# Four PSUM banks by turns, head-by-head maxima and a new order of slots in a fused routing attention and feed-forward kernel

## The chip, the core and the metric

The kernel runs on one core of a Trainium2 chip. Five engines work side by side, each through its own list of instructions in order: TensorE (PE, matrix products; its weight loads appear as PEld), VectorE (DVE), ScalarE (ACT), GpSimd (POOL), and SyncE (SP), which here only issues transfers. They wait for each other through semaphores. Matrix products are written to PSUM, which this kernel divides into eight banks; all else is in SBUF. The metric is the device time of one execution in microseconds (us). The kernel before takes 1357.56 us, the median of three runs (1356.3 to 1358.26).

## What is computed

An attention block with 4 batches, 8 heads, 768 positions and head width 64, and then a feed-forward block on its 3072 x 512 result. A query sees only the keys that fall to the same one of 16 centroids:

```python
q_assign = np.argmax(np.einsum('bhsd,hcd->bhsc', q_n, c_n), axis=-1)
k_assign = np.argmax(np.einsum('bhsd,hcd->bhsc', k_n, c_n), axis=-1)
mask = q_assign[:, :, :, None] == k_assign[:, :, None, :]
scores = scale * np.matmul(q, k.transpose(0, 1, 3, 2))
scores = np.where(mask, scores, -1000000000.0)
scores = scores - np.max(scores, axis=-1, keepdims=True)
attn = np.exp(scores)
attn = attn / (np.sum(attn, axis=-1, keepdims=True) + 1e-09)
out = np.matmul(attn, v)
# ... and then, x being out as (3072, 512):
h = x @ w_in                                                # 512 -> 2048
sp = np.maximum(h, 0.0) + np.log1p(np.exp(-np.abs(h)))      # softplus
return (h * erf(sp)) @ w_out                                # 2048 -> 512
```

q, k, v and the centroids arrive as 32-bit floats. The two weight matrices arrive as 64-bit floats and are rebuilt as 32-bit ones on the chip.

## The kernel before

The kernel works on pairs of heads, 16 of them, four to a batch. A pair has 12 **units**, each a block of 128 keys against half of the queries (384), for both heads. The parts that matter:

The memory pools in PSUM. A tile of ps_s takes two banks, all others take one, so these pools are all eight banks:

```python
ps_s = pool("ps_s", 2, space=PSUM)     # sc (scores) and sm (maxima)
ps_v = pool("ps_v", 1, space=PSUM)     # av, attention times v
ps_t = pool("ps_t", 1, space=PSUM)     # psim, pn, psum: small things
ps_f = pool("ps_f", 2, space=PSUM)     # hp, po: feed-forward; av2
```

The weights are rebuilt in 32 **steps**, 16 for w_in and 16 for w_out. Each has a load, ACT's absolute value, two POOL operations (clamp and bias), and five DVE instructions, one to a call of `prepare(1)`:

```python
def clamp(n):
    ae.activation(out=x, in_=hi, func=ACT.Abs)
    ge.tensor_scalar(out=x, in0=x, scalar1=TINY_HI, scalar2=None, op0=ALU.max)
    ge.tensor_tensor(out=x, in0=x, in1=bias.to_broadcast([P, LC]), op=ALU.add)
def convert():
    ...
        ve.tensor_scalar(out=m, in0=x, scalar1=3, scalar2=None, op0=ALU.logical_shift_left); yield
        # ... fetch of a later step
        ve.tensor_scalar(out=x, in0=m, scalar1=0x7F800000, scalar2=None, op0=ALU.bitwise_and); yield
        # ... clamp of a later step
        ve.scalar_tensor_tensor(out=xf, in0=lo, scalar=2.0**-52, in1=xf, op0=ALU.mult, op1=ALU.mult); yield
        ve.tensor_tensor(out=xf, in0=mf, in1=xf, op=ALU.add); yield
        ve.scalar_tensor_tensor(out=w_steps[n][0], in0=hi, scalar=0x80000000, in1=x, ...); yield
```

`route(p)` finds the clusters of pair p and writes one-hot rows into the operands qm and km, which add the mask to the scores; `shift(p)` finds each query's maximum and writes its negative into one row of qm. Both are prepared while the pair before is worked on (`aside`):

```python
def route(p):                       # each yield ends one portion
    # DVE: transposes of q and k -> qT, kT; load of the next pair
    yield
    # PE: psim = similarities; ACT: copies of qT, kT into qm, km
    yield
    ve.transpose(out=sims, in_=psim)
    ve.reduce_max(out=mx, in_=sim, axis=AX.X)
    ve.tensor_tensor(out=sim, in0=sim, in1=mx..., op=ALU.is_equal)
    ge.tensor_tensor(out=sim, in0=sim, in1=rank..., op=ALU.mult)
    # ACT: the row of shifts is set to 0
    yield
    ve.reduce_max(out=mr, in_=sim, axis=AX.X)
    # DVE: hot (two halves), hotT = its transpose; DVE -> qm, ACT -> km
    yield
def shift(p):
    for t in range(NJ):             # 6 blocks of queries
        for half in range(2):       # halves of the keys
            sm = ps_s.tile([P, 2, 512], F32, name="sm", tag="s")
            for e in range(2):      # the two heads
                te.matmul(sm[:, e, 0:HW], lhsT=st["qm"]..., rhs=st["km"]..., start=True, stop=True)
            ve.tensor_reduce(out=nmx[:, t, half], in_=sm[:, :, 0:HW], axis=AX.X, op=ALU.max, negate=True)
            yield
    # nm = min of both halves (DVE), pn = its transpose (PE), nmT (ACT),
    # and through DRAM (line) into the row of qm, all queries at once
    yield
```

A unit is scored (`scores`: products into sc, exponential into pr by ACT, the sum acc over units by POOL), multiplied with v two units later (`attend`: av) and divided after six (`divide`: psum by PE, logarithm and exponential by ACT, den and xT by DVE). The feed-forward has 12 chunks of 256 positions: `hidden` fills hp, DVE copies it to g; `gate` multiplies g with erf(softplus(g)); `project` fills po, which DVE copies to osb:

```python
def gate(n):
    for i in range(2): ae.activation(out=s[i], in_=h[...], func=ACT.Softplus)
    for i in range(2): ae.activation(out=s[i], in_=s[i], func=ACT.Erf)
    for i in range(0, NFT, GW):     # eight pieces
        ve.tensor_tensor(out=h[:, i : i + GW], in0=s[...], in1=h[:, i : i + GW], op=ALU.mult)
```

The first batch is laid out in slots, in which every engine keeps the order of the program; from slot FIRST on a scheduler may move instructions, and the feed-forward (`pump`) is mixed in:

```python
FIRST = 2 * NJ * HP - 4
for slot in range(-2 * NJ, 2 * NJ * HP):     # -12 .. 47; one unit to a slot
    in_order[0] = slot < FIRST
    p, r = divmod(slot + 2 * NJ, 2 * NJ)
    if slot >= 0:
        scores([slot])
    if r == 0:
        ready[p] = aside(p)
    prepare(3 if slot < 0 else (1, 3, 1)[r] if r < 3 else 3 if r > 9 else 0)
    for _ in range(1 if r < 4 or r == 10 else 2 if r < 10 else 0):
        next(ready[p])
    if slot >= 2:
        # ... second part of an earlier divide
        attend(slot - 2, ...)
        # ... divide after six units
    if slot >= FIRST:
        pump(4 * NFT * TB)
```

After it, units 48 to 191 go two at a time; each two have five rounds of `pump(per_slot)`, `prepare(2)` and, where ASIDE lists the round, one portion of the next pair's preparation. What is left of the feed-forward runs at the end.

Of the kernel before, what the change touches and what calls it, by code (L numbers as in the profile page):

```python
# [17 lines left out]
P = 128  # L18
# [11 lines left out]
GW = 2  # L30
# [13 lines left out]
ASIDE = (0, 2, 4, 6, *range(9, 9 + 2 * NJ), 10 + 2 * NJ)  # L44
FIRST = 2 * NJ * HP - 4
# [19 lines left out]
def kernel(  # L65
# [33 lines left out]
    ps_v = pool("ps_v", 1, space=PSUM)  # L99
    ps_t = pool("ps_t", 1, space=PSUM)  # L100
    ps_f = pool("ps_f", 2, space=PSUM)
# [51 lines left out]
    load_qk(0)  # L153
# [42 lines left out]
    room = [gp.tile([P, NFT, TB], F32, name="g") for _ in range(2)]  # L196
# [3 lines left out]
    def fetch(n):  # L200
        if n in steps or n >= len(w_steps):
            return
        if n < n_w_in:
            t = room[n // 2 % 2][:, n % 2 * (NFT // 2) : (n % 2 + 1) * (NFT // 2)]
        else:
            t = half_tile()
        t = t.rearrange("p f t -> p (f t)").bitcast(U32)
        nc.sync.dma_start(out=t[:, 0 : 2 * LC], in_=w_steps[n][1])
        raw = t[:, 0 : 2 * LC].rearrange("p (n w) -> p n w", w=2)
        steps[n] = raw[:, :, 1], raw[:, :, 0], t[:, 2 * LC : 3 * LC], t[:, 3 * LC : 4 * LC]  # L210
# [53 lines left out]
    for n in range(3):  # L264
        fetch(n)
# [33 lines left out]
    pct = ps_t.tile([P, P], F32, name="pct", tag="t")  # L299
# [12 lines left out]
    def route(p):  # L312
# [9 lines left out]
        psim = ps_t.tile([P, HW], F32, name="psim", tag="t")  # L322
# [21 lines left out]
        )  # L344

# [3 lines left out]
        for e in range(2):  # L349
            row = low["q"][e * D + SH : e * D + SH + 1, e]  # L350
            ae.mul(out=row, in_=row, mul=0.0)
# [11 lines left out]
        ve.transpose(out=hotT, in_=hot)  # L363
        for half in range(2):
            cols = slice(half * HW, (half + 1) * HW)
            for e in range(2):
                r = slice(e * D, e * D + Q)
                g = slice(half * Q, (half + 1) * Q)
                ve.tensor_scalar_mul(out=low["q"][r, e, cols], in0=hotT[g], scalar1=own[g, e : e + 1])
                g = slice(D + half * Q, D + (half + 1) * Q)  # L370
                ae.copy(out=low["k"][r, e, cols], in_=hotT[g])
# [4 lines left out]
    def shift(p):  # L376
        st = pairs[p]
        nmx = small.tile([P, NJ, 2, 2], F32, name="nmx")
        load(p, "v", v, vp)
        for t in range(NJ):  # L380
            for half in range(2):
                sm = ps_s.tile([P, 2, 512], F32, name="sm", tag="s")
                for e in range(2):
                    te.matmul(
                        sm[:, e, 0:HW], lhsT=st["qm"][:, e, t * P : (t + 1) * P],
                        rhs=st["km"][:, e, half * HW : (half + 1) * HW], start=True, stop=True,
                    )
                ve.tensor_reduce(
                    out=nmx[:, t, half], in_=sm[:, :, 0:HW], axis=AX.X, op=ALU.max, negate=True
                )  # L390
                yield
        nm = small.tile([P, 2, NJ], BF16, name="nm")
        ve.scalar_tensor_tensor(
            out=nm.rearrange("p e t -> p t e"), in0=nmx[:, :, 0], scalar=FLOOR, in1=nmx[:, :, 1],
            op0=ALU.min, op1=ALU.min,
        )
        pn = ps_t.tile([2 * NJ, P], BF16, name="pn", tag="t")
        te.transpose(out=pn, in_=nm.rearrange("p e t -> p (e t)"), identity=identb)
        nmT = small.tile([2 * NJ, P], BF16, name="nmT")
        ae.copy(out=nmT, in_=pn)  # L400
        line = linep.tile([2 * NJ, P], BF16, name="line")
        nc.sync.dma_start(out=line, in_=nmT)
        for e in range(2):
            r = e * D + SH
            nc.sync.dma_start(
                out=st["qm"][r : r + 1, e],
                in_=line[e * NJ : (e + 1) * NJ].rearrange("(o t) p -> o (t p)", o=1),
            )
        yield
# [8 lines left out]
    def scores(us):  # L418
# [13 lines left out]
        for u, sc in zip(us, tiles):  # L432
            p, half, j = units[u]
            st = pairs[p]
            for e in range(2):
                r = slice(e * D, (e + 1) * D)
                te.matmul(
                    sc[:, e, 0:HW], lhsT=st["km"][r, e, j * P : (j + 1) * P],
                    rhs=st["qm"][r, e, half * HW : (half + 1) * HW], start=False, stop=True,
                )  # L440
            pr = prs[u % NPT]
            ae.activation(out=pr[:, :, 0:HW], in_=sc[:, :, 0:HW], func=ACT.Exp, scale=D**-0.5)

            if j == 1:
                st["acc", half] = accp.tile([P, 2, HW], F32, name="acc")
                ge.tensor_tensor(
                    out=st["acc", half], in0=prs[(u - 1) % NPT][:, :, 0:HW], in1=pr[:, :, 0:HW], op=ALU.add
                )
            elif j > 1:
                ge.tensor_tensor(  # L450
                    out=st["acc", half], in0=st["acc", half], in1=pr[:, :, 0:HW], op=ALU.add
                )

    def attend(u, other=False):
# [3 lines left out]
        if j == 0:  # L458
            st["av", half] = (
                ps_f.tile([P, HW + 2], F32, name="av2", tag="f") if other  # L460
                else ps_v.tile([P, HW + 2], F32, name="av")
            )
# [6 lines left out]
    def divide(u):  # L469
# [5 lines left out]
        psum = ps_t.tile([P, HW], F32, name="psum", tag="t")  # L475
        for e in range(2):
            te.matmul(
                psum[e * D : (e + 1) * D], lhsT=minus, rhs=st["acc", half][:, e], start=True, stop=True
            )

# [33 lines left out]
    def gate(n):  # L514
# [6 lines left out]
        for i in range(2):  # L521
            ae.activation(out=s[i], in_=s[i], func=ACT.Erf)
        for i in range(0, NFT, GW):
            ve.tensor_tensor(
# [6 lines left out]
    def hidden(n):  # L531
        b, c = n // CPB, n % CPB
        gs[n] = gp.tile([P, NFT, TB], F32, name="g")
        for fp in range(NFT // GW):
            while converted[0] < DM // P * ((fp + 1) * GW * P // LC):
                yield None
            hp = ps_f.tile([P, GW, TB], F32, name="hp", tag="f")
# [17 lines left out]
    def project(n):  # L555
        b, c = n // CPB, n % CPB
        for tt in range(TJ):
            po = ps_f.tile([P, DM], F32, name="po", tag="f")
# [60 lines left out]

    ready = {}  # L620
    for slot in range(-2 * NJ, 2 * NJ * HP):
        in_order[0] = slot < FIRST
        p, r = divmod(slot + 2 * NJ, 2 * NJ)
        if slot >= 0:
            scores([slot])
        if r == 0:
            ready[p] = aside(p)
        prepare(3 if slot < 0 else (1, 3, 1)[r] if r < 3 else 3 if r > 9 else 0)

        for _ in range(1 if r < 4 or r == 10 else 2 if r < 10 else 0):  # L630
            next(ready[p])
        if slot >= 2:
            if (slot - 2) % NJ == 0 and slot > 2:
                next(part)
            attend(slot - 2, other=(slot - 2) // NJ % 2 == 1 and slot < FIRST - 2)
            if (slot - 2) % NJ == NJ - 1:
# [4 lines left out]
    for u in range(2 * NJ * HP - 2, 2 * NJ * HP):  # L641
        attend(u)
    for _ in divide(2 * NJ * HP - 1):
        pass
    in_order[0] = False
# [4 lines left out]
    for u in range(2 * NJ * HP, len(units), 2):  # L650
# [8 lines left out]
        scores([u, u + 1])  # L659
        for i in range(SLOTS):  # L660
# [42 lines left out]
```

## Time and profile before

| | busy us | share of the span |
|---|---|---|
| PE | 1179.2 | 87% |
| PEld | 620.3 | 46% |
| DVE | 657.4 | 49% |
| ACT | 553.8 | 41% |
| POOL | 396.2 | 29% |

The profiled execution spans 1355.1 us with 12573 instructions. The shares are averages over stages with different limits. Of the costliest groups of instructions, the matmuls of hp keep PE busy for 380.5 us, those of po for 376.4, those of sc for 180.5 and 60.6, av 151.2, sm 104.9. On DVE the reductions of sm take 181.1 us (192 of them), the gate's product 69.2 (96), the copies of hp 65.8 (96). On POOL the sums acc take 224.2 and 60.0. Transfers keep the 16 DMA engines busy 13.8% of the span. A row of the timeline gives start, duration, engine, operation, tiles, number of instructions merged, and in brackets how long the engine stood idle before it and who released it; every helper call has the same line (L56), so groups are told apart by their tiles. A busy PE is not PE at its peak: matmuls overlap, and the ends of their records are modelled.

### The profile page before, as it was taken

How to read it: one execution, taken by the hardware profiler on the slowest of the kernel's cores; microseconds unless marked ns; L12 is line 12 of the kernel's file. 1: busy time of each engine (PE TensorE's matmuls, PEld its weight loads, DVE VectorE, ACT ScalarE, POOL GpSimd, SP SyncE). 2: the span in 40 equal slices, each digit the busy share in tenths (PEclk: the TensorE clock that was granted, in tenths of full speed). 3: DMA queues.
4: the chain of work that ended last, by engine and by line, in shares of the span. 5: the costliest groups of instructions: out<-in, count | busy, mean ns of one | idle time of the engine just before them, and what ended most of it. 6: DMA issues, size and time to landing. Idle time of an engine off the chain costs nothing.

```text
span 1355.1 us, 12573 instructions
## 1 busy us (share of the span) xinstructions
PE 1179.2 (87%) x4881; PEld 620.3 (46%) x4881; DVE 657.4 (49%) x958; ACT 553.8 (41%) x626; POOL 396.2 (29%) x262
## 2 busy tenths in 40 slices
PE   1376866987878999899999899999999999999998
PEld 0122222464423545345645545546546446575764
DVE  7956759449686345634444535435444513121221
ACT  4144334272651337444616535525527227130311
POOL 6445545226353222422222222222212122100000
PEclk9987978998879999899999999999999899999999
DMA  6413302031131102020201010101100000000000
GB/s 152 131 28 67 66 1 35 1 66 62 47 86 43 24 20 43 1 43 8 36 8 32 12 32 20 24 20 24 20 9 21 0 8 8 8 8 8 8 16 15
DMA packets 134156, 42.89 MB, mean 32 GB/s; under 512 B 126896, under 2 KB 126928, under 8 KB 134096
## 3 DMA queue, kind: packets, MB, share of 16 engines
q1 hardware_dynamic: 134096, 42.09, 13.8%
q8 instruction: 38, 0.62, 0.2%
q14 instruction: 22, 0.18, 0.0%
HBM read 35.73 MB, written 6.34 MB: 31 GB/s over the span
## 4 chain that ended last, share of the span: by engine, by line
PE 54%; DVE 19%; ACT 13%; issue 8%; POOL 4%; DMA 1%; ACTq 0%; SPq 0%; DVEq 0%; POOLq 0%
PE po L56 21%; PE hp L56 16%; PE sc L56 7%; DVE g L56 5%; PE av L56 5%; DVE nmx L56 4%; PE sm L56 3%; ACT L56 3%; ACT a_s L56 3%; ACT pr L56 2%; DVE a_s L56 2%; ACT inv L56 2%; ACT km L56 2%; DVE den L56 2%; ACT qm L56 1%
## 5 line engine op out<-in xcount | busy, mean ns | idle before, releaser
L56 PE MATMUL hp<-xT,w_in 128*128 128x256 f32 x1536 | 380.5, 387 | 14.5 <-DVE g L56 12.3
L56 PE MATMUL po<-w_out,g 128*128 128x512 f32 x768 | 376.4, 611 | 14.0 <-DVE w_out L56 11.5
L56 POOL TENSOR_TENSOR acc<-acc,pr 128x768 f32<-128x768 f32 x128 | 224.2, 1752 | 473.9 <-ACT pr L56 458.4
L56 PEld LDWEIGHTS hp<-xT,w_in 128*128 128x128 f32 x1536 | 288.2, 192 | 126.4 <-issue 70.7
L56 ACT ACTIVATE pr<-sc 128x768 f32<-128x768 f32 x192 | 148.1, 808 | 323.8 <-PE sc L56 323.4
L56 DVE TENSOR_REDUCE nmx<-sm 128x2 f32<-128x768 f32 x192 | 181.1, 954 | 146.0 <-PE sm L56 144.9
L56 PEld LDWEIGHTS po<-w_out,g 128*128 128x128 f32 x768 | 142.8, 193 | 132.3 <-issue 102.7
L56 PE MATMUL sc<-qT,kT 64*128 64x384 f32 x768 | 180.5, 556 | 17.2 <-DVE nmx L56 11.5
L56 PE MATMUL sm<-km,qm 128*128 128x384 bf16 x384 | 104.9, 355 | 75.5 <-ACT km L56 31.4
L56 ACT ACT_TABLE_LOAD x112 | 143.7, 1283 | 57.1 <-issue 47.0
L56 DVE COPY g<-hp 128x512 f32<-128x512 f32 x96 | 65.8, 687 | 198.4 <-PE hp L56 198.4
L56 PE MATMUL av<-pr,in_v 128*64 128x386 f32 x768 | 151.2, 511 | 0.0
L56 POOL TENSOR_TENSOR acc<-pr,pr 128x768 f32<-128x768 f32 x32 | 60.0, 1875 | 215.3 <-ACT pr L56 215.3
L56 PEld LDWEIGHTS sc<-qT,kT 64*128 64x128 f32 x768 | 68.0, 197 | 115.3 <-issue 50.5
L56 PEld LDWEIGHTS <-qm 128*128 128x128 bf16 x384 | 36.1, 101 | 158.4 <-issue 137.6
L56 ACT ACTIVATE a_s<-g 128x2048 f32<-128x2048 f32 x24 | 45.8, 1910 | 139.3 <-DVE g L56 139.1
L56 DVE TENSOR_TENSOR g<-a_s,g 128x512 f32<-128x512 f32 x96 | 69.2, 779 | 43.3 <-ACT a_s L56 43.1
L56 PEld LDWEIGHTS av<-pr,in_v 128*64 128x64 f32 x768 | 50.3, 139 | 77.8 <-issue 76.5
L56 DVE SCALAR_TENSOR_TENSOR den<-psum,inv 128x384 f32<-128x384 f32 x32 | 17.8, 557 | 129.3 <-ACT inv L56 129.2
L56 ACT COPY km<-hotT 32x384 bf16<-32x384 bf16 x64 | 32.5, 508 | 88.2 <-DVE hotT L56 87.4
L56 PE MATMUL sc<-qm,km 64*128 64x384 bf16 x384 | 60.6, 341 | 5.3 <-DMA qm<-line 5.3
L56 ACT ACTIVATE a_s<-a_s 128x2048 f32<-128x2048 f32 (+1 forms) x40 | 56.6, 1415 | 20.9 <-DMA a_s<-in_moe_w_out_dram 20.6
(69 smaller groups left out, 691.8 us busy)
## 6 DMA issues: line engine op xcount, KB each, us to landing
g<-in_moe_w_in_dram SPq DMA_DIRECT2D x16, 512.0 KB
a_s<-in_moe_w_out_dram SPq DMA_DIRECT2D x16, 512.0 KB
in_q<-in_q_dram SPq DMA_DIRECT2D x64, 96.0 KB
in_k<-in_k_dram SPq DMA_DIRECT2D x64, 96.0 KB
in_v<-in_v_dram SPq DMA_DIRECT2D x32, 192.0 KB
out_dram<-osb SPq DMA_DIRECT2D x24, 256.0 KB
qm<-line SPq DMA_DIRECT2D x32, 1.5 KB
line<-nmT SPq DMA_DIRECT2D x16, 3.0 KB
```

What stands on the lines that cost most here:

```text
L56: ins = getattr(self.engine, name)(*args, **kw)
```

## The change

It has six parts, which all aim at waits of one engine for another.

1. **Banks.** The pools ps_v, ps_t and ps_f become one pool of four banks, ps_x, whose tiles go to whichever of the four is free. Only scores keep ps_s to themselves; sm moves to ps_x.
2. **Maxima head by head.** A tile of sm holds one head (128 x 384) in place of two, so there are 24 reductions of 384 elements for a pair in place of 12 of 768.
3. **Shift by halves.** The maxima of the first 384 queries are sent to the row of qm while those of the second are still worked out; each half has its own nm, pn, nmT and three transfers.
4. **Slots in another order.** A table, `plan`, says how many portions of the preparation come before the scores of a slot, how many after, and how many DVE instructions of the weights. The routing is cut into more portions. The accumulation of a unit on POOL comes one slot later. Far fewer weight steps stand ahead of slot 0.
5. **Gate's product on POOL**, for all chunks but the last.
6. **Staging of weights.** w_in is staged in one g tile and two half tiles in place of two g tiles; the first transfer of a weight goes ahead of those of q and k. The feed-forward asks for w_in by what it reads.

```diff
-ASIDE = (0, 2, 4, 6, *range(9, 9 + 2 * NJ), 10 + 2 * NJ)
-FIRST = 2 * NJ * HP - 4
+ASIDE = (0, 1, 3, 4, 6, 8, *range(11, 11 + NJ), 12 + NJ, *range(14 + NJ, 14 + 2 * NJ), 15 + 2 * NJ)
+FIRST = 2 * NJ * HP - 3
...
-    ps_v = pool("ps_v", 1, space=PSUM)
-    ps_t = pool("ps_t", 1, space=PSUM)
-    ps_f = pool("ps_f", 2, space=PSUM)
+    ps_x = pool("ps_x", 4, space=PSUM)
...
-    for n in range(3):
-        fetch(n)
+    fetch(0)
+    load_qk(0)
+    fetch(1)
+    fetch(2)
...  # shift(p), inner loops
+        for h in range(2):
+            ts = slice(h * HJ, (h + 1) * HJ)
+            for t in range(h * HJ, (h + 1) * HJ):
+                for half in range(2):
+                    for e in range(2):
+                        sm = ps_x.tile([P, HW], F32, name="sm", tag="x")
+                        te.matmul(sm, lhsT=..., rhs=..., start=True, stop=True)
+                        ve.tensor_reduce(
+                            out=nmx[:, half, e, t : t + 1], in_=sm, axis=AX.X, op=ALU.max, negate=True
+                        )
+                    yield
+            # nm, pn, nmT, line and the row of qm for this half
+            yield
...
+        engine = ge if n < NCHUNK - 1 else ve
         for i in range(0, NFT, GW):
-            ve.tensor_tensor(
+            engine.tensor_tensor(
...
-            while converted[0] < DM // P * ((fp + 1) * GW * P // LC):
+            while converted[0] < DM // P * (fp * GW * P // LC + 1):
...
+    plan = (          # portions before, after; weight instructions in the prologue, later
+        (1, 0, 5, 0), (1, 0, 3, 4), (1, 0, 1, 0), (1, 0, 2, 0), (1, 0, 1, 2), (0, 2, 0, 0),
+        (0, 2, 0, 0), (0, 2, 0, 0), (0, 2, 2, 0), (0, 2, 0, 1), (0, 2, 0, 1), (0, 1, 1, 2),
+    )
...
+        before, after, *ops = plan[r]
+        next(part, None)
+        for _ in range(before):
+            next(ready[p])
         if slot >= 0:
             scores([slot])
+        prepare(ops[p > 0])
+        if r == 0 and p > 0:
+            next(ready[p - 1])
+        for _ in range(after):
+            next(ready[p])
+        next(part, None)
+        if slot > 0:
+            accumulate(slot - 1)
+        if r == 2:
+            next(ready[p])
         if slot >= 2:
-            attend(slot - 2, other=...)
+            attend(slot - 2)
```

## The prediction, made before the changed kernel ran

> **What bounds the kernel now.** I read the row of slices first, then busy time by stage, then the timeline inside the worst stages, then the waits of the best one. The first view, the page's slices, says that there are two kernels in one:
>
> ```profile
> PE   1376866987878999899999899999999999999998
> DVE  7956759449686345634444535435444513121221
> PEclk9987978998879999899999999999999899999999
> ```
>
> From the sixteenth slice on PE is at 9 of 10; before it PE is at 6 to 8 on a reduced clock, and in the first two slices it hardly works. To find the borders I counted ScalarE's exponentials (pr<-sc, 192 of them, 12 to a pair of heads) along the timeline. Numbers 0, 12, 24, 36, 48, 60, 84, 96 and the last start at about 66, 114, 162, 208, 294, 385, 526, 580 and 1160 us. Busy time in those stages (columns: window, its length, then busy us and count for PE, PEld, DVE, ACT, POOL, then clock, DMA share, GB/s):
>
> ```profile
> 0.00:66.00 66.00, 14.90 (x42) 4.57 (x44) 55.57 (x110) 16.58 (x24) 37.74 (x43) 1.00 0.56 141
> 66.00:114.00 48.00, 36.05 (x152) 11.20 (x151) 31.33 (x42) 19.20 (x28) 24.15 (x15) 0.82 0.21 42
> ...
> 208.00:294.00 86.00, 68.57 (x317) 37.02 (x313) 48.37 (x66) 43.01 (x47) 25.38 (x16) 0.94 0.18 30
> 294.00:462.00 168.00, 138.41 (x526) 70.50 (x526) 118.19 (x161) 67.12 (x83) 76.36 (x50) 0.88 0.22 59
> ...
> 580.00:1160.00 580.00, 552.96 (x2406) 303.46 (x2404) 244.54 (x353) 266.08 (x292) 148.41 (x87) 0.99 0.10 19
> 1160.00:1355.00 195.00, 191.42 (x634) 116.40 (x634) 37.42 (x58) 43.43 (x30) 3.36 (x2) 1.00 0.03 11
> ```
>
> What a pair needs of PE I take from dense stretches in the chain of waits: two units of scores (12 records) 1.82 us, six units of av (24 records) 4.04 us; a sum tile psum 0.81; two sm about 0.42 from start to start. A pair is then 12 x 0.91 + 12 x 0.67 + 24 x 0.21 + 2 x 0.81 + about 0.9 for psim = 26.5 us, and the three pairs between 66 and 208 us take 48, 48 and 46. Half of that stage is therefore lost, and no engine is full in it: PE 36, DVE 31, POOL 24 of 48 us. It is bound by waits. The timeline shows which. In the prologue and in the fourth pair:
>
> ```profile
> 33.90 1.66 PE L56 MATMUL sm<-km,qm 128*128 128x384 bf16 x4 [1.78 <-DVE nmx L56]
> 38.12 1.66 PE L56 MATMUL sm<-km,qm 128*128 128x384 bf16 x4 [2.56 <-DVE nmx L56]
> ...
> 65.51 0.65 PE L56 MATMUL sc<-qm,km 64*128 64x384 bf16 x2 [3.84 <-DMA qm<-line]
> ...
> 174.57 0.99 POOL L56 TENSOR_TENSOR sims<-sims,rank 128x384 f32<-128x384 f32 x1
> 175.60 0.55 DVE L56 TENSOR_REDUCE mr<-sims 128x24 f32<-128x384 f32 x1 [4.31 <-POOL sims L56]
> ...
> 179.38 1.01 PE L56 MATMUL sm<-km,qm 128*128 128x384 bf16 x2 [8.23 <-ACT km L56]
> ```
>
> Prologue: two tiles of sm fill the two score buffers, DVE reduces them, then does conversion steps of the weights that stand between the reductions in program order, and PE waits about 2.5 us in every 4. At its end the row of shifts goes through DRAM in one piece (3.84 us). Later: POOL reaches the routing product sims only at 174.57, after an accumulation and a weight clamp, and PE stands 8.23 us because the scores of the next unit are ordered behind sm.
>
> **What the Trainium skill says.** "Perfetto Trace Analysis", Optimizing Tensor Performance, Matmuls: independent matmul groups should rotate through different PSUM banks, so that the evacuation of one overlaps the next group. The prologue above is the lack of it. "SBUF — State Buffer", Who interferes with whom: a DVE instruction with two SBUF inputs contends with a POOL instruction that reads SBUF; tensor_reduce never does. The trace agrees: the reductions have a steady mean of 954 or 955 ns, while nm, two SBUF inputs of 12 elements, took 0.19 us once and 1.67 us beside an accumulation. "GPSIMD Engine Reference", Performance versus the Vector engine: a two-input elementwise operation costs about 1.96 times DVE's. Here POOL's 128x384 product takes 0.993 us and its 128x768 sum 1.73 to 1.77; half way, 128x512, I estimate 1.3 us to DVE's 0.78 (mean of the page).
>
> **The change part by part.** The order of instructions in the built programs shows what the diff alone doesn't.
>
> *Prologue, -20 us.* Nine conversion steps stand before the first exponential now, three after the change. A step is five DVE instructions, 0.42 + 0.42 + 3 x 0.69 = 2.9 us undisturbed; six fewer are 17 us of a DVE that is busy 55.6 of 66. The routing starts right after the transposes instead of behind a conversion, and the two halves of the shifts overlap the trip through DRAM, worth the 3.84. Against that 24 reductions of one head (0.55 us, as for the 128x384 reductions mr and mx) replace 12 of two heads (0.95): +1.8. From the order I rebuild: routing product at 23 to 24 us (it stands behind four clamps whose weights must land), sm at 28, 24 reductions to 45, first exponential at about 46 in place of 66.
>
> *Three pairs, units 0 to 36, -25 us.* sm leaves the score buffers, scores and accumulations of older units go ahead of it, and the routing is cut into one link per slot. DVE sets the floor: 92.7 us over the three pairs is 31 each, plus 1.9 for the split reductions and 1.2 for a second nm, 34. PE is 26.5 at a clock near 0.85, so 31. The chain of routing (transposes 1.9, psim 1, three DVE steps 1.9, POOL 1 to 2.7, mr to hotT 3, copies 2.1: 12 to 14 us in slots 0 to 4) and seven slots of about 2.9 us give 34 to 37. I take 39 for a pair, 117 for 142.
>
> *Units 36 to 48, -14 us.* Ten conversion steps fall here after the change, three now. Beside POOL a step costs 2 x 0.70 + 0.93 + 0.94 + 0.90 = 4.2 us (groups of DVE, 66 to 208 us). DVE: 10 x 4.2 + (34 - 2 x 4.2) = 68, so about 72 for 86. Only 32 matmuls hp run here in place of 61; 29 x 0.44 = 13 us move on.
>
> *Units 48 to 96, +3 us.* Both programs enter with 18 or 19 steps done and leave with the same number of hp and po behind them. The 13 us that moved in meet a stage that is not full (168 us for units 48 to 72, DVE 118); two gates leave DVE (16 x 0.78 = 12 us) and land on POOL. I count +3.
>
> *Units 96 to 192, -8 us.* Placing of the feed-forward is the same unit for unit. PE's waits here:
>
> ```profile
> PE hp L56 <- DVE g L56: 7.4, 4, 2.0
> PE sm L56 <- DVE nmx L56: 5.8, 2, 2.9
> PE sm L56 <- ACT pr L56: 4.6, 5, 1.7
> ...
> PE pn L56 <- DVE nm L56: 2.1, 3, 1.3
> ```
>
> They are those that more banks and a gate off DVE can take, 20 us with sc's; I count 8, because sm, av, psum and po will now want the same four banks. The tail has nothing to give.
>
> Sum: 1357.6 - 20 - 25 - 14 + 3 - 8 = 1293.6, so **1293 us**.
>
> **Rivals.** *A bank shortage takes the place of the old wait.* In the built order one sm after each psum waits for the bank that den frees, and in PE's order only about 3 us lie between, while table loads, logarithm, exponential and den take 4.2 (1.28 + 0.58 + 1.28 + 0.52 + 0.56). For it: two such places in a pair. Against: the same place already waits for pr now (1.67 us at 1009). If each costs 2 us more, 8 pairs lose 32 and the result is about 1325. *POOL becomes the bound.* Its product adds 88 x 1.3 = 114 us to 396, and DVE's two-input work waits behind it. Against: POOL is at 26% between 580 and 1160 us, and the second half of a gate comes some 24 us after the first (738 and 762), so po has slack. It would cost 10 to 20 us. *The conversion is only moved.* Then prologue and first pairs gain, and units 36 to 96 give back as much: 1315 to 1330. For it: 32 steps are the same 93 to 134 us of DVE wherever they stand. *The pairs reach DVE's floor* of 34 us: 1275.
>
> **Range and chances.** The prologue is the surest term (15 to 24 us), the pairs next (15 to 40), the stretch from 36 to 96 the least sure (30 lost to 30 gained). Together 1262 to 1324. A result within 2% needs 1330 or more, that is, more than half of the gain given back; slower than 2% needs a shortage of banks everywhere. Faster 0.92, same 0.06, slower 0.02.
>
> **What would show it.** First exponential near 46 us; pairs of about 39 us, with no wait of sm on km above 3 us; unit 48 near 235; DVE above 80% from 46 to 235; unit 96 near 525; then a steady part of about 572 us in which hp's waits on g are gone. I am wrong if PE's waits on den, xT or po's copies exceed 20 us in the steady part, if the pairs stay above 44, or if units 48 to 96 exceed 310.

## The result and the profile after

The changed kernel takes **1326.47 us**, median of four runs (1325.09 to 1327.52), against 1357.91 us for the kernel before in the same session. The ratio is 0.977, with a 95% interval of 0.975 to 0.979: faster by 2.3%, about half of the predicted gain and 2.5 us above the predicted range.

The page of the changed kernel, rows of 40 slices:

```profile
PE   1687767897749999899999999999999999999998
...
DVE  7777798558647335534434444335334322110121
...
PEclk9898887898958999999999999999999999999999
```

PE starts earlier (6 instead of 3 in the second slice), but the tenth to twelfth slices (7, 7, 4) are now the hole of the program. Busy time by stage, borders at exponentials 0, 36, 48, 60, 72, 96 and 191 (columns: window, length, busy us and count for PE, PEld, DVE, ACT, POOL, then clock, DMA share, GB/s):

```profile
44.00:174.00 130.00, 99.03 (x474) 31.17 (x474) 98.11 (x172) 59.22 (x88) 66.94 (x43) 0.88 0.26 50
174.00:255.30 81.30, 56.93 (x231) 25.41 (x231) 66.10 (x104) 28.48 (x40) 42.56 (x29) 0.83 0.25 61
255.30:331.40 76.10, 66.16 (x302) 41.82 (x303) 48.16 (x77) 42.73 (x51) 40.32 (x28) 0.91 0.21 52
331.40:434.30 102.90, 74.36 (x256) 31.75 (x254) 60.76 (x96) 39.94 (x48) 52.86 (x37) 0.80 0.23 57
434.30:571.30 137.00, 130.93 (x582) 70.74 (x581) 60.62 (x107) 62.84 (x75) 47.20 (x30) 1.00 0.12 24
571.30:1132.20 560.90, 544.05 (x2385) 300.19 (x2385) 216.75 (x395) 262.93 (x294) 203.52 (x133) 0.99 0.09 19
```

PE is the engine that everything must pass, so length minus PE's busy time is what a stage loses. With the same borders in the kernel before:

| stage | before: length, PE idle | after: length, PE idle | change of length | predicted |
|---|---|---|---|---|
| prologue | 66.2, 51.1 | 44.0, 29.6 | -22.2 | -20 |
| units 0 to 36 | 142.1, 37.6 | 130.0, 31.0 | -12.1 | -25 |
| units 36 to 48 | 86.2, 17.9 | 81.3, 24.4 | -4.9 | -14 |
| units 48 to 72 | 167.7, 29.1 | 179.0, 38.5 | +11.3 | } +3 |
| units 72 to 96 | 125.6, 9.5 | 137.0, 6.1 | +11.4 | } |
| units 96 to 191 | 572.9, 27.0 | 560.9, 16.9 | -12.0 | -8 |
| tail | 194.4, 3.7 | 193.5, 3.7 | -0.9 | 0 |

(The prediction put exponential 96 of the kernel before at 580 us and exponential 84 at 526; counting every one gives 587.8 and 536.1, and the table uses these. The predicted changes do not rest on it.) In these runs the change is worth 29.4 us where 64 were predicted. Units 48 to 96 fall short by 19.7 us, units 0 to 36 by 12.9 and units 36 to 48 by 9.1; the other three rows came out 7.1 us better together. In units 36 to 72 PE does 9.4 us less work than before (197.5 against 206.9) and the stretch is still 6.4 us longer. In units 72 to 96 PE does 14.8 us more, in a stage where it was full already: at unit 72 the kernel before has 296 matmul records of hp and 76 of po behind it, the changed one 256 and 54, and at unit 96 both have 424 and 143. Longer matmuls are not the reason: in units 48 to 72 a record of hp takes 398 ns and one of po 681, against 407 and 712 before.

The timeline of the changed kernel, second pair. Each pair of rows is GpSimd with the VectorE work beside it; then the wait it leads to:

```profile
87.40 5.26 POOL L56 TENSOR_TENSOR acc<-acc,pr 128x768 f32<-128x768 f32 x3
89.18 3.76 DVE L56 TENSOR_SCALAR g<-g 128x512 uint32<-128x512 uint32 x2
...
100.33 3.62 POOL L56 TENSOR_TENSOR acc<-acc,pr 128x768 f32<-128x768 f32 x2
100.98 3.38 DVE L56 TENSOR_TENSOR hot<-sims,mr 64x384 bf16<-64x384 f32 x2
105.56 1.54 PE L56 MATMUL sm<-km,qm 128*128 128x384 bf16 x3 [4.41 <-ACT km L56]
```

Two weight instructions that take 0.42 us each when alone take 3.76 together, and the two comparisons of the routing (0.56 each alone) take 3.38. The three waits of sm on km in this stage are 5.2, 4.4 and 4.4 us, 14.0 together, where they were 19.0 before (8.23 the longest). The chain from the transposes (87.4) to the first sm (105.6) is 18 us long; before it took 17, 18 and 21 us in the three pairs.

The same kernel at the gate of the second chunk:

```profile
374.33 9.83 POOL L56 TENSOR_TENSOR g<-a_s,g 128x512 f32<-128x512 f32 x8 [10.80 <-ACT a_s L56]
379.30 5.23 SPq L206 DMA_DIRECT2D a_s<-in_moe_w_out_dram  x2
384.12 3.42 POOL L56 TENSOR_TENSOR acc<-acc,pr 128x768 f32<-128x768 f32 x2
389.06 2.93 PE L56 MATMUL sc<-qT,kT 64*128 64x384 f32 x8 [6.83 <-ACT pr L56]
390.15 1.70 DVE L56 TENSOR_SCALAR a_s<-a_s 128x512 uint32<-128x512 uint32 x2 [14.03 <-POOL a_s L56]
```

The eight products fill GpSimd for 9.83 us. The next weights of w_out are fetched into a_s, the tiles that the gate uses, once the products have freed them; then GpSimd does two sums before the clamp, and VectorE stands 14.03 us. In units 48 to 72 VectorE waits 41.7 us for GpSimd's a_s, after (first) and 9.3 before:

```profile
DVE a_s L56 <- POOL a_s L56: 41.7, 7, 14.0
...
DVE a_s L56 <- POOL a_s L56: 9.3, 5, 3.3
```

The gate of the first chunk shows what became of the head start. Its last four products stand here between the last instructions of two weight steps that follow one another; the first three rows are of the kernel before, the others of the changed one:

```profile
224.38 0.69 DVE L56 SCALAR_TENSOR_TENSOR w_out<-a_s 128x512 uint32<-128x512 uint32 x1
292.81 2.50 DVE L56 TENSOR_TENSOR g<-a_s,g 128x512 f32<-128x512 f32 x4 [7.09 <-ACT a_s L56]
311.82 0.69 DVE L56 SCALAR_TENSOR_TENSOR w_out<-a_s 128x512 uint32<-128x512 uint32 x1
...
255.10 0.69 DVE L56 SCALAR_TENSOR_TENSOR w_out<-a_s 128x512 uint32<-128x512 uint32 x1
293.12 4.95 POOL L56 TENSOR_TENSOR g<-a_s,g 128x512 f32<-128x512 f32 x4 [7.51 <-ACT a_s L56]
311.16 0.68 DVE L56 SCALAR_TENSOR_TENSOR w_out<-a_s 128x512 uint32<-128x512 uint32 x1
```

In both kernels the weight steps pause around this gate until about 312 us. But unit 48 starts at 294.5 us before and at 255.3 after, so a pause that lay mostly ahead of unit 48 now lies behind it. The last step ends at 428.0 us before and at 423.7 after: of the 39.2 us won up to unit 48 the conversion keeps 4.3. Both kernels have 18 of the 32 steps done at unit 48; from there the other 14 took 133.5 us before and take 168.4 now.

The largest of PE's waits in units 96 to 191:

```profile
PE sm L56 <- DVE xT L56: 4.2, 4, 1.1
PE sm L56 <- DVE den L56: 3.6, 4, 1.6
```

The 7.4 us of hp on g are gone. PE's waits on den and xT, whose reads free the shared banks, are now 12.1 us in five rows (0.7 before), most of the 16.9 us in which PE is idle in this stage.

### The profile page after: what moved, and what is told of

Its sections match the earlier page's. It is cut to its first block, busy times and chain, and to the rows that moved or that the text cites. A ratio compares the mean times of both kernels' runs of the same rounds, so it can differ in the third digit from the quotient of the medians.

```text
span 1325.7 us, 12944 instructions
## 1 busy us (share of the span) xinstructions
PE 1175.7 (89%) x4897; PEld 621.2 (47%) x4897; DVE 612.9 (46%) x1078; ACT 552.3 (42%) x640; POOL 500.0 (38%) x350
## 4 chain that ended last, share of the span: by engine, by line
PE 60%; DVE 14%; ACT 10%; POOL 8%; issue 6%; DMA 1%; SPq 0%; DVEq 0%; ACTq 0%; POOLq 0%
PE po L56 24%; PE hp L56 18%; PE sc L56 8%; PE av L56 6%; PE sm L56 4%; POOL g L56 3%; DVE nmx L56 3%; DVE a_s L56 3%; ACT L56 3%; ACT a_s L56 2%; DVE den L56 2%; POOL a_s L56 2%; POOL acc L56 2%; DVE hot L56 2%; ACT km L56 1%
## 5 line engine op out<-in xcount | busy, mean ns | idle before, releaser
L56 DVE TENSOR_REDUCE nmx<-sm 128x1 f32<-128x384 f32 x384 | 194.8, 551 | 147.6 <-PE sm L56 146.3
L56 PEld LDWEIGHTS po<-w_out,g 128*128 128x128 f32 x768 | 142.7, 192 | 123.3 <-issue 102.0
L56 PE MATMUL sc<-qT,kT 64*128 64x384 f32 x768 | 177.2, 543 | 22.4 <-ACT pr L56 22.4
L56 POOL TENSOR_TENSOR g<-a_s,g 128x512 f32<-128x512 f32 x88 | 110.6, 1289 | 206.0 <-ACT a_s L56 206.0
L56 PE MATMUL sm<-km,qm 128*128 128x384 bf16 x384 | 112.4, 356 | 80.2 <-ACT km L56 21.9
L56 ACT ACTIVATE a_s<-a_s 128x512 f32<-128x512 f32 (+1 forms) x48 | 61.6, 1290 | 66.5 <-DMA a_s<-in_moe_w_out_dram 51.3
L56 DVE TENSOR_SCALAR a_s<-a_s 128x512 uint32<-128x512 uint32 x48 | 39.3, 822 | 48.4 <-POOL a_s L56 48.0
L56 POOL TENSOR_SCALAR a_s<-a_s 128x512 f32<-128x512 f32 x24 | 37.5, 1563 | 60.0 <-ACT a_s L56 60.0
```

What stands on the lines that cost most here:

```text
L56: ins = getattr(self.engine, name)(*args, **kw)
```

## The experiments

In all runs the edit stands alone against the changed kernel, unless said otherwise. Stage lengths are from the one profiled execution; in five runs it lay well under the median of its kernel (by 7 us in the second, 9 in the fifth, 4 to 5 in the fourth, eleventh and fourteenth), so totals are judged by medians and only large stage differences by the stages. Up to unit 48, runs 1, 2 and 13 have the changed kernel's instructions in its order, and units 36 to 48 still take 78.3, 79.1 and 78.6 us in them, and 81.3 in the changed kernel.

| run | median | prologue | units 0-36 | 36-96 | 96-191 |
|---|---|---|---|---|---|
| before | 1357.9 | 66.2 | 142.1 | 379.5 | 572.9 |
| after | 1326.5 | 44.0 | 130.0 | 397.3 | 560.9 |
| 1 gate on VectorE | 1322.4 | 45.2 | 128.7 | 392.9 | 559.7 |
| 2 the same, two chunks | 1321.7 | 44.2 | 130.2 | 387.8 | 557.1 |
| 3 more steps in the prologue | 1334.7 | 60.3 | 132.5 | 384.5 | 560.5 |
| 4 steps off the routing | 1319.0 | 44.6 | 123.8 | 391.2 | 560.5 |
| 5 runs 2 and 4 | 1323.8 | 45.0 | 123.3 | 394.2 | 557.2 |
| 6 most sums left out | 1297.7 | 45.2 | 121.7 | 375.9 | 558.9 |
| 7 sm with the scores | 1337.7 | 45.2 | 129.7 | 405.2 | 561.4 |
| 8 three banks | 1442.2 | 45.5 | 148.9 | 409.2 | 637.6 |
| 9 clamp on VectorE | 1308.8 | 41.6 | 125.7 | 385.0 | 561.0 |
| 10 before, with the banks | 1344.3 | 66.4 | 143.7 | 384.0 | 554.8 |
| 11 runs 4 and 9 | 1303.5 | 41.5 | 132.5 | 370.5 | 558.6 |
| 12 first two gates left out | 1309.0 | 43.7 | 129.0 | 380.2 | 558.5 |
| 13 twelve steps cut short | 1292.7 | 45.0 | 129.1 | 364.7 | 558.5 |
| 14 run 11, product dealt out | 1307.4 | 40.2 | 135.6 | 374.2 | 557.1 |

### 1 and 2: whose is the gate's product?

```diff
-        engine = ge if n < NCHUNK - 1 else ve
+        engine = ve                                      # run 1
+        engine = ge if 1 < n < NCHUNK - 1 else ve        # run 2
```

> The changed kernel (1326.5 us) with the gate's product back on VectorE for all chunks; all else is kept. Theory A (the product on POOL, eight pieces in one stretch of about 10 us, stands before the clamps of the weights and the accumulations while the conversion still runs, and holds its two staging tiles): units 48 to 96 take 8 to 15 us less than the 316.0 of the changed kernel, above all units 60 to 72 (102.9), and the steady part, units 96 on, takes 4 to 8 us more, as hp waits on g again; sum 1318 to 1324. Rival B (the conversion was only moved, POOL is innocent): units 48 to 96 within 3 us of 316.0, the steady part 4 to 8 us longer; sum 1329 to 1333.

> The changed kernel with the product of the gate on VectorE for the first two chunks alone, those that fall beside the conversion of the weights; the later chunks stay on POOL. Theory A: units 48 to 96 shorten by 8 to 15 us and the steady part stays at 561, so 1312 to 1319. Rival B: nothing is gained in units 48 to 96, so 1325 to 1328.

Both gained some 4 to 5 us by the median: ratios to before 0.974 (0.972 to 0.976) and 0.972 (0.969 to 0.975). The intervals just touch that of the changed kernel, but no execution of either (at most 1323.2 us) reaches its fastest (1325.1). With all products on VectorE, units 96 to 191 take 559.7 us against 560.9: GpSimd's help there is worth nothing. The loss is a fraction of the theory's 8 to 15 us. It fits that units 60 to 72, where the second product lies, take 98 us in place of 102.9, but a difference of this size in one stage is not proof of the place (3.0 of run 1's 4.4 us fall in units 36 to 48, ahead of the first product). Theory A holds in direction, not in size; part 5 of the change costs some 4 us.

### 3: is the conversion only moved?

```diff
-        (1, 0, 5, 0), (1, 0, 3, 4), (1, 0, 1, 0), (1, 0, 2, 0), (1, 0, 1, 2), (0, 2, 0, 0), ...
+        (1, 0, 5, 0), (1, 0, 3, 4), (1, 0, 2, 0), (1, 0, 3, 0), (1, 0, 3, 2), (0, 2, 3, 0), ...
```

> The changed kernel with 36 weight instructions of VectorE in the prologue in place of 15, so that some four more steps of the conversion are done before the first exponential. Theory B (the gain of the prologue is in good part a debt, paid back in units 36 to 96): the first exponential comes 15 to 18 us later than the 44.0 of the changed kernel, units 36 to 96 take 12 to 22 us less than 397.3, and the sum is 1320 to 1330. Rival (the late stretch is bound by other things, such as the order of POOL's work): the prologue loses as much and units 36 to 96 shorten by less than 5 us, sum about 1340.

The prologue grew by 16.3 us and units 36 to 96 shrank by 12.8; with 2.5 us more in the pairs the total is 8.2 us worse. Some four steps cost 16.3 us in the prologue and 12.8 us in units 36 to 96: most of that part of the prologue's gain is a debt, and the sum lies between both expectations.

### 4 and 5: weight steps out of the routing slots

```diff
-        (1, 0, 3, 4), ... (1, 0, 1, 2), (0, 2, 0, 0), (0, 2, 0, 0), (0, 2, 0, 0), (0, 2, 2, 0), (0, 2, 0, 1), ...
+        (1, 0, 3, 0), ... (1, 0, 1, 0), (0, 2, 0, 1), (0, 2, 0, 1), (0, 2, 0, 1), (0, 2, 2, 1), (0, 2, 0, 2), ...
```

> The changed kernel with the ten weight instructions of a pair taken out of the slots in which the routing runs (the second and the fifth) and put into the slots after it; as many in all. Theory C (the pairs of 42.5 to 44.4 us are too long because weight instructions of VectorE stand beside an accumulation of POOL, take 3.4 to 3.8 us for two in place of 0.84, and hold up the chain of the routing): the three pairs take about 40 us each, the wait of sm on km drops from 14.0 us for three to below 6, sum about 1317. Rival (the pairs are at VectorE's floor): no pair changes by more than 1 us, sum within 2 us of 1326.5.

Ratio to before 0.971 (0.969 to 0.974); pairs of 41.3 us. The timeline of this kernel at the place shown above:

```profile
95.89 2.51 DVE L56 TENSOR_TENSOR hot<-sims,mr 64x384 bf16<-64x384 f32 x2
...
100.11 0.89 PE L56 MATMUL sm<-km,qm 128*128 128x384 bf16 x3 [1.37 <-ACT km L56]
```

From the transposes (85.5) to the first sm it takes 14.6 us now, and the three pairs' waits on km fell from 14.0 to 5.8 us. Theory C is confirmed for 2 us a pair. The comparisons still stretch (2.51 us for two).

> The changed kernel with both edits of before at once: the gate's product on VectorE for the first two chunks, and the weight instructions of the pairs moved out of the slots of the routing. If the two losses are separate (one falls in units 60 to 72, the other in units 0 to 36), they add: 1326.5 - 4.8 - 7.5 = 1314, 1311 to 1317. If both act through the same thing, VectorE waiting for GpSimd's clamps in units 48 to 72, the second adds nothing to the better of the two: 1318 to 1321.

Run 5 was no better than run 4: 1323.8 us, with executions from 1315 to 1330. That the two gains add (1314 us) is not borne out; with this spread it is unclear whether the second gain is there at all.

### 6: what GpSimd's sums cost the others

```diff
-        elif j > 1:
-            ge.tensor_tensor(out=st["acc", half], in0=st["acc", half], in1=pr[:, :, 0:HW], op=ALU.add)
```

> The changed kernel with the sums over units left out from the third unit of a half on (four of five accumulations on GpSimd; the softmax denominators then lack those units). It sizes what GpSimd's sums cost the others. Theory C (beside a sum, VectorE's weight instructions and the two comparisons of the routing take several times their length, and GpSimd's own clamps stand behind sums): the three pairs fall from 43.3 to 37 to 39 us each, units 36 to 96 by 15 to 30 us, sum 1280 to 1300. Rival (the pairs and the stretch after are bound by the chains of PE, ScalarE and VectorE alone, and the sums are hidden): pairs lose less than 1.5 us each and the sum is 1315 to 1326.

The total fits the theory (1297.7), and so do units 36 to 96 (21.4 us less). The pairs do not: 40.6 us where 37 to 39 were expected, little below run 4. The instructions that stood beside sums are short again, two weight instructions and the two comparisons in the second pair:

```profile
86.88 0.88 DVE L56 TENSOR_SCALAR g<-g 128x512 uint32<-128x512 uint32 x2
...
98.76 1.12 DVE L56 TENSOR_TENSOR hot<-sims,mr 64x384 bf16<-64x384 f32 x2
```

They took 3.76 and 3.38 us beside sums. Even so a pair needs 16 us from the transposes to the first sm and then 25 for the rest. Most of what is left of a pair is thus not due to the sums.

### 7 and 8: maxima in the score buffers; a bank less

```diff
-                    for e in range(2):
-                        sm = ps_x.tile([P, HW], F32, name="sm", tag="x")
+                    sm = ps_s.tile([P, 2, 512], F32, name="sm", tag="s")
+                    for e in range(2):      # two products, then one reduction of 768 elements
```

> The changed kernel with the maxima as before it: sm holds two heads in one of the two score buffers, and 12 reductions of 768 elements replace 24 of 384; the other tiles keep the four shared banks. If moving sm out of the score buffers is what shortened the prologue and the pairs: first exponential 3 to 6 us later, pairs 46 to 47 us instead of 43.3, steady part 3 to 8 us longer, sum 1340 to 1350. Rival (the new order of slots and fewer weight steps did it, and the split reductions only cost VectorE 1.8 us a pair): the pairs keep 42 to 43 us and the sum is 1320 to 1328.

A surprise: with sm back in the score buffers the first exponential comes 1.2 us later, the pairs take 43.2 us and units 96 to 191 change by 0.5. What I had named as a means of the prologue and of the pairs does nothing there. Nearly all of what it is worth (7.9 of 9.3 us in the profiled runs) falls in units 36 to 96.

```diff
-    ps_x = pool("ps_x", 4, space=PSUM)
+    ps_x = pool("ps_x", 3, space=PSUM)
```

> The changed kernel with three shared PSUM banks instead of four; the eighth bank stays unused. If the steady part gained its 12 us from a choice of banks (and not from the gate, which the gate's run already says), taking one away returns most of it: units 96 to 191 take 568 to 580 us instead of 561, the pairs 1 to 3 us more each, sum 1337 to 1352. Rival (three banks are enough, as PE waits for banks only 17 us in the steady part): within 4 us of 1326.5.

It costs 116 us, where 11 to 26 were expected: 19 in the pairs, 77 in units 96 to 191. Of these 77 only 22 are idle time of PE (38.9 us in place of 16.9); the rest is counted as busy time, for the same number of matmuls, at a granted clock of 0.96 in place of 0.99, and is not explained. The bank shortage of the prediction is one bank away.

### 9: GpSimd out of the weight steps

```diff
-            ge.tensor_scalar(out=x, in0=x, scalar1=TINY_HI, scalar2=None, op0=ALU.max)
-            ge.tensor_tensor(out=x, in0=x, in1=bias.to_broadcast([P, LC]), op=ALU.add)
+            ve.tensor_scalar(out=xf, in0=xf, scalar1=TINY_HI, scalar2=None, op0=ALU.max)
+            ve.tensor_scalar(
+                out=x, in0=x, scalar1=0x0FFFFFFF, scalar2=0x08000000,
+                op0=ALU.bitwise_and, op1=ALU.bitwise_xor,
+            )
```

> The changed kernel with the clamp and the subtraction of the exponent's bias taken off GpSimd: VectorE does them as two one-input operations (a maximum, and a mask with an exclusive or that gives the same bits) ahead of the shift, so a weight step goes from ScalarE straight to VectorE. VectorE gets 32 x 2 x 0.42 = 27 us more (nearer 40 beside GpSimd's sums), GpSimd 32 x 2.5 = 80 us less. Theory D (units 48 to 96 grew because the conversion that was moved there passes through GpSimd, behind sums and the gate's product; VectorE waited 41.7 us for GpSimd between units 48 and 72): units 48 to 72 fall from 179.0 to 155 to 168, VectorE's waits on GpSimd's a_s are gone, pairs within 2 us of 43, sum 1305 to 1318. Rival (VectorE itself is the bound of the early part): pairs 45 to 46, units 36 to 48 90 or more, sum 1330 to 1350.

Although VectorE has more to do, the total fell to 1308.8 us, ratio to before 0.964 (0.963 to 0.966). The total is in the expected range, the place was another. Units 36 to 48 of this kernel:

```profile
167.30:239.80 72.50, 54.78 (x246) 24.94 (x246) 65.29 (x117) 29.53 (x44) 20.01 (x12) 0.88 0.28 65
```

They take 72.5 us in place of 81.3 with the same busy time of VectorE (65.3 and 66.1): the difference is waiting. But units 48 to 72 lost only 3.4 of their 179.0 us, and the timeline at the gate shows why:

```profile
348.55 9.84 POOL L56 TENSOR_TENSOR g<-a_s,g 128x512 f32<-128x512 f32 x8 [13.33 <-ACT a_s L56]
...
353.52 5.23 SPq L206 DMA_DIRECT2D a_s<-in_moe_w_out_dram  x2
...
356.80 0.66 ACT L56 ACTIVATE a_s<-a_s 128x512 f32<-128x512 f32 x1 [3.70 <-DMA a_s<-in_moe_w_out_dram]
357.49 1.18 DVE L56 TENSOR_SCALAR a_s<-a_s 128x512 f32<-128x512 f32 x1 [8.69 <-ACT a_s L56]
```

GpSimd no longer stands in the chain, but the tiles do: the weight that VectorE waits 8.69 us for was fetched when the gate's first four products had released a_s (353.5). VectorE's waits on the weights in units 48 to 72, 41.7 us for GpSimd in the changed kernel, are 20.9 us for ScalarE here. This gave the theory G of runs 12 to 14.

### 10: the banks alone, on the kernel before

```diff
-    ps_v = pool("ps_v", 1, space=PSUM)
-    ps_t = pool("ps_t", 1, space=PSUM)
-    ps_f = pool("ps_f", 2, space=PSUM)
+    ps_x = pool("ps_x", 4, space=PSUM)     # av, av2, psum, psim, pn, hp, po
```

> The kernel before (1357.6 us) with the banks of the change alone: one pool of four banks for av, psum, psim, pn, hp and po in place of pools of 1, 1 and 2; sm stays in the score buffers, order, gate and maxima are as before. If the steady part gained its 12 us by the free choice of banks: units 96 to 191 take 558 to 564 us in place of 572.9, the earlier part stays within 4 us of 587.8, sum 1343 to 1348. Rival (the later accumulation, the shift by halves and the new places of the preparation did it): the steady part within 3 us of 572.9, sum 1354 to 1360.

Ratio to before 0.990 (0.989 to 0.992). Units 96 to 191 of this kernel:

```profile
594.10:1148.90 554.80, 540.77 (x2379) 298.44 (x2378) 239.88 (x352) 261.75 (x287) 144.25 (x85) 1.00 0.09 18
```

They lose 18.1 us, more than the whole change takes from them (12.0), and more than expected; the part ahead of unit 96 grew by 6.3, where less than 4 was expected. The free choice of banks is enough to explain the gain of this stage; in the whole change some 6 us of it are lost again. The gate (run 1) and the place of sm (run 7) are not what loses them. In run 7 PE's waits on den and xT are 3.5 us in place of 12.1, and the stage takes 561.4 all the same. Which of the remaining differences of order does was not tried.

### 11: both remedies

The edits of runs 4 and 9 together.

> The changed kernel with the clamp on VectorE and the weight instructions of the pairs moved out of the slots of the routing, together; a candidate for the best version. If the two losses are separate, 1319 less the 8 to 20 us of the clamp: 1300 to 1312. If the one-input operations beside GpSimd's sums stretch to 1.7 us each and VectorE becomes the bound of slots 5 to 11: pairs 44 to 46 us, sum 1320 to 1335.

This is the fastest of the kernels that leave nothing out: 1303.5 us (1298.4 to 1306.3), ratio to before 0.960 (0.957 to 0.962), 23 us under the changed kernel. Units 36 to 72, in three windows:

```profile
174.00:243.40 69.40, 54.59 (x245) 25.08 (x245) 62.99 (x110) 29.08 (x43) 18.97 (x12) 0.90 0.28 62
243.40:319.20 75.80, 63.03 (x289) 41.96 (x289) 57.62 (x97) 37.27 (x43) 29.32 (x19) 0.91 0.22 61
319.20:407.60 88.40, 70.37 (x256) 30.56 (x254) 67.73 (x116) 41.51 (x49) 28.81 (x19) 0.88 0.27 68
```

PE's idle time here is 233.6 - 188.0 = 45.6 us, against 62.8 in the changed kernel and 47.0 in the one before. The pairs grew to 44.2 us; a weight step now has seven VectorE instructions instead of five, in the slots after the routing. Both expectations hold in part.

### 12 to 14: the gate or the conversion?

```diff
-            if fp == NFT // GW - 1:
+            if fp == NFT // GW - 1 and n > 1:      # run 12: chunks 0 and 1 stay without a gate
                 gate(n)
```

> The changed kernel with the gate of the first two chunks left out (their hidden values go ungated into the second product; 2 x 4 ScalarE instructions of about 1.85 us, their table loads and 16 products of 1.2 us are missing). Theory G (the gate takes both staging tiles of the weights, so no weight is fetched until its last product is done, and ScalarE runs it ahead of exponentials): units 36 to 96 take 370 to 380 us in place of 397.3, nearly all of it in units 48 to 72, sum 1300 to 1310. Rival (the conversion's own length sets that stretch): less than 8 us are won, sum 1318 to 1325.

Units 36 to 96 took 380.2 us, 17.1 less, at the edge of what theory G named, and the total fell to 1309.0 us. The gain starts at unit 60: units 60 to 72 take 84.2 us instead of 102.9.

```diff
+            if n >= 20:                            # run 13: load and one VectorE instruction only
+                fetch(n + 1)
+                ve.scalar_tensor_tensor(out=w_steps[n][0], in0=hi, scalar=0x80000000, in1=hi, ...)
+                converted[0] = n + 1; yield; continue
```

> The changed kernel with the last twelve weight steps cut to their load and one VectorE instruction (w_out then holds raw bit patterns in those rows; four VectorE, two GpSimd and one ScalarE instruction a step are left out). The theory that the conversion's length is the bound: 12 steps at the 3 us each that four steps in the prologue were worth are 36 us, so units 48 to 96 take 280 to 290 in place of 316.0, sum 1290 to 1300. Theory G (loads wait for the staging tiles that the gate holds, and PE for its work): 8 to 18 us are won, sum 1308 to 1318.

Units 48 to 96 took 286.1 us and the total was 1292.7, as the theory of the conversion's length has it: 2.5 us to a step in this stretch, 2.8 in the total. Units 60 to 72 of runs 12 and 13 beside each other:

```profile
334.30:418.50 84.20, 66.85 (x266) 32.04 (x264) 51.53 (x81) 22.29 (x34) 35.07 (x23) 0.88 0.17 50
```

```profile
324.60:398.60 74.00, 70.96 (x297) 36.54 (x295) 31.66 (x59) 37.78 (x41) 28.39 (x19) 0.98 0.25 62
```

Without the conversion PE is idle for 3.0 of 74.0 us although the gates run; without the gates it is still idle for 17.4 of 84.2. So the two theories are not rivals: the conversion is the bound of this stretch, and the gates among its steps lengthen it. Whether they do so by holding the tiles or by their own work on ScalarE and GpSimd, run 12 does not tell, as both are gone in it.

```diff
-            engine.tensor_tensor(
+            (ve if n < 2 and i // GW % 2 else engine).tensor_tensor(      # run 14, on run 11
```

> The version with the clamp on VectorE and weight steps off the routing (1303.5 us), and the eight products of the first two gates dealt out in turn to GpSimd and VectorE, so that the staging tiles are free sooner. Theory G: the product of the second chunk ends 3 to 5 us sooner, the next weights land as much sooner, sum 1295 to 1301. Rival (both engines are held up by each other, or the tiles are waited for by nobody): within 3 us of 1303.5.

1307.4 us (1302.4 to 1310.0); its ratio, 0.963 (0.961 to 0.966), lies above that of run 11 with overlapping intervals. The next two views, of run 14 and then of run 2, show the product of the second chunk:

```profile
350.51 2.37 DVE L56 TENSOR_TENSOR g<-a_s,g 128x512 f32<-128x512 f32 x2
350.56 6.79 POOL L56 TENSOR_TENSOR g<-a_s,g 128x512 f32<-128x512 f32 x4 [12.40 <-ACT a_s L56]
353.27 2.96 DVE L56 TENSOR_TENSOR g<-a_s,g 128x512 f32<-128x512 f32 x2
```

```profile
369.80 4.91 DVE L56 TENSOR_TENSOR g<-a_s,g 128x512 f32<-128x512 f32 x8 [4.42 <-ACT a_s L56]
```

VectorE alone does eight products in 4.91 us; both together need 6.84. The tiles were free 3 us sooner than with GpSimd alone (9.84 in run 9) and the total did not gain. That speaks against the holding of the tiles as what the second gate costs.

## Why the prediction was wrong

**Prologue: right.** First exponential at 44.0 us (46 predicted). Its explanation was half right: fewer steps ahead of slot 0 give 16.3 of the 22.2 us (run 3), the new place of sm does not (run 7), so PE's waits on nmx there were not a want of banks. The shift by halves and the order of loads were not tried alone.

**Pairs: right mechanism, wrong size.** They are bound in part by waits on the routing, as said, but the sign that these would be gone, no wait of sm on km above 3 us, did not come (4.4 to 5.2). Two terms were too small. The chain "12 to 14 us" measured 18: I had added undisturbed durations, while weight instructions and comparisons stand beside GpSimd's sums. The Trainium skill ("SBUF — State Buffer", Who interferes with whom) says that a VectorE instruction in a two-port mode contends with GpSimd, and that whoever issues first gets the shared ports for the whole instruction. The trace fits it, with 0.42 us turned into 1.93 and 1.79 beside a sum and 0.44 without one (run 6); that this is such a mode no run shows directly. Run 4 takes 3.6 us out of the chain and 2.1 out of a pair. And the seven slots of "about 2.9 us" take 25 us in place of 20.3, even without the sums (run 6); why is open, and so is which part of the new order won the 12.1 us of this stage.

**Units 36 to 48: the busy time was right, the length was not.** VectorE was busy 66.1 us, 68 predicted. The failed step is "so about 72": it took the length to be VectorE's busy time and 4 us. A weight step goes through a load, ScalarE, GpSimd and VectorE, and VectorE stood 15 us, 6.3 of them for GpSimd's a_s. With GpSimd out of that chain the stage took 72.5.

**Units 48 to 96: the step that failed.** "The 13 us that moved in meet a stage that is not full" gave +3; it was +22.7. PE and VectorE had idle time there, but it was not room: the length of units 48 to 72 is mainly that of the weight steps and of the gates among them. With the steps cut short PE is idle for 3.0 us in units 60 to 72 instead of 28.5 (run 13), and with the first two gates left out units 36 to 96 are 17.1 us shorter (run 12). I had taken equal counts of steps, hp and po at both ends as proof of balance. The counts were right, but they leave out the pause of the steps at the first gate (from 225.1 to 312.5 us before, from 255.8 to 311.8 after): the head start of 39.2 us put unit 48 ahead of it, and so the last 14 steps take 168.4 us from unit 48 in place of 133.5. In run 12 there is no such pause (steps end at 255.0, 269.2 and 292.1 us), and the last step ends 135.6 us after unit 48 starts. GpSimd's hold on the chain adds to it: its gate products some 4 us (runs 1 and 2), its part in the steps and its sums more (runs 9 and 6 lose 12 and 21 us in units 36 to 96). How the 22.7 us divide between these causes is not shown, as no run takes the gates out of the kernel before. What PE could not do in time went to units 72 to 96, where it was full (+14.8 us of work, +11.4 of time).

**Units 96 to 191: right for one of two reasons.** The banks do it (run 10). The gate does not: with the product back on VectorE hp still does not wait on g, and the stage takes 559.7 us (run 1).

**The rivals.** "The conversion is only moved", put at 1315 to 1330, came nearest in the number; run 3 shows how much is moved. Its account holds by half: units 36 to 96 gave back 17.8 of the 34.3 us that the prologue and the pairs gained, and not because more steps fall behind unit 48 (18 are done there in both kernels). GpSimd as bound was right for 4 to 5 us. The shortage of banks came in part only: PE's waits on den and xT are 12.1 us in the steady part, under the 20 that were set for it, and run 8 shows how near it was. Of the conditions set for being wrong, the one on units 48 to 96 (over 310 us; 316.0) came true, and the first pair just touched another (over 44 us; 44.3, then 43.2 and 42.5).

## What to carry to other kernels

Account for a stage by its bound engine's idle time, and before moving work into that idle time ask what chain sets the stage's length: time in which everybody waits is not room. Work of the bound engine that leaves a loose stage for a full one costs most of its length there (11.4 of 14.8 us here). Equal counts at the border of a stage are no proof of balance: find the pauses in which nothing is counted, such as a gate among weight steps, and see on which side of the border they fall.

## What was not expected of the hardware

- Dealing two-input products of 128 x 512 to both engines was slower than VectorE alone: 6.84 against 4.91 us for eight. In the first two gates a product takes 1.71 to 1.78 us on GpSimd beside VectorE, and on VectorE three of eight take 0.69 and five 1.28 to 1.76; alone they take 0.69 and 1.27 (medians of the groups).
- One PSUM bank fewer for the shared tiles cost 116 us of 1326, although with four banks PE's waits on the instructions that free them came to some 12 us in units 96 to 191 (of its 17 of idle time).
